# Attention of the second batch moved from the head into the first expert unit

## The chip, the cores and the metric

The kernel runs on one core of one Trainium2 chip. The metric is the device time of one execution in microseconds. Times before: 521.01 us median of three runs (519.59 to 523.30). The engines are called as the profile calls them: PE (TensorE; PEld is its weight load), DVE (VectorE), ACT (ScalarE), POOL (GpSimd), SP (SyncE, which issues most DMAs). Each engine works through its own instructions in order.

## The reference

Two blocks follow one another. The first is a cross attention between 512 tokens and 32 states for each of 8 batches and 8 heads of 64; it is computed both ways:

```python
scores  = scale * x @ state.T;   a  = softmax(scores);   xread = a  @ state    # tokens read states
scores2 = scale * state @ x.T;   a2 = softmax(scores2);  sread = a2 @ x        # states read tokens
out = concatenate([xread, sread], axis=2)          # 544 rows per batch and head
```

Its output, as 8 x 544 rows of 512, goes into a layer of 8 experts. A row takes the expert with its largest logit, or, where a local gate is open, the expert of the row before it in the batch; the first row of a batch always takes its own:

```python
e = fresh_e if s == 0 or local_gate[b, s] < 0.5 else prev_e
h = relu(x[b, s] @ w1[e]);   out[b, s] = softmax(logits[b, s])[e] * (h @ w2[e])
```

All is in fp32. One expert has 2 MB in `w1` (512 x 1024) and 2 MB in `w2`.

## The kernel before

**Units and tiles.** Each batch's 512 token rows are multiplied by the expert of that batch's first row: eight *units*. The 32 state rows of each batch go by their own experts: all 256 are sorted by expert into at most nine *tiles* of 32 rows (`Tile`, line 920), which need 2 MB + 2 MB of weights each. What fits neither is done at the end under a condition that does not come true with these data.

**A unit.** The two matrix products of a unit are done by a scheme of seven products of quarters instead of eight. It needs sums of the operands beforehand: four over the tokens (`column_sum`, line 842), four over the first weights (`first_sum`, line 831), four over the second (`second_sum`, line 847), all on DVE, line 829. A unit is two halves of the first multiplication (`first_half`, n = 0 and 1, products of line 1041) and two of the second (`second_half`, products of line 1088), each of seven products of eight matmuls: 28 products. The first product of a half needs no sums, the second needs the first sum of each kind. After each product `tick()` is called and whatever has been put at that number is issued: the order of the work beside the products is written out by hand in ticks. Unit u has ticks 28u + 1 to 28u + 28 (`PER = 28`). At the end of each half, places 4u to 4u + 3, `bound` may put in the first (`one`, line 950) or second multiplication (`two`, line 963) of a state tile.

**Attention.** A batch is a list of some 40 steps named by two letters: `sc` scores (PE, line 299), `tr` transposes to states and `mo` maxima over them, `sb`, `ex`, `zh`, `zs`, `zi`, `ml`, `tb` the softmax over states, `mx`, `nb`, `et`, `tu`, `ec`, `iv` that over tokens, `sr` state reads (PE, line 382, reads the rows `x_n`), `st`, `rt`, `ws`, `sl`, `sk` the state results, their rows to memory and their logits, `lg`, `lt` logits of tokens, `vv` token reads (PE, line 427), `xr`/`xd` their copies, `wr` their way to memory (`xts`), `fe` the first row's expert. `kp` are matmuls on zeros that keep PE going. `HEAD` gives the order for batches 0 and 1 ahead of the first unit; `FLOW` gives that of a batch b from 2 on, in ticks counted from `FIRST + PERIOD * (b - 2)`. Batch 0's token reads stay in SBUF as the first unit's tokens; for others `load_x` (line 822) reads them back from `xts`. A batch's tokens come in two layouts, `x_t` and `x_n`, 1 MB each, into one buffer each once the head is over.

**Routing.** `choose` (line 535) finds experts and probabilities for a group of batches in seven parts, put at seven ticks; its fourth part is a scan over 544 positions on DVE and its fifth takes the result to PE. `route` (line 607) sorts the states. Groups are batches 0 and 1, 2 to 4, 5 to 7.

**Queues.** SP issues in program order and waits in that order for what an issue needs. Writes to `out` go by indirect DMAs on POOL: for each half of the second multiplication two scatters of 128 rows (`scatter`, line 1023, data `y`), and one of line 972 for a tile (data `yt`, one buffer). Each waits for the one before it to land, except that the two scatters of the last half of all are declared independent of each other.

## Time and profile before

| | |
|---|---|
| median of three runs | 521.01 us (519.59 to 523.30) |
| profiled execution | 519.18 us |
| its span, first to last instruction | 516.9 us |
| granted PE clock, mean | 0.993 |
| busy: PE, DVE, ACT, POOL | 495.2, 278.1, 161.1, 109.3 us |
| moved by DMA | 115.67 MB, 224 GB/s over the span |
| first product of unit 0 | starts at 29.21 us |

A row of the order of time has the start in microseconds from the span's beginning, the duration, the engine, line and operation, what is written and read (names of tiles), shapes and count, and in brackets the idle time of the engine before it and what ended that. Rows in a row of the same kind are merged. A row of windows has the stretch, its length, busy time of PE, PEld, DVE, ACT and POOL with counts, the granted PE clock, the busy share of the DMA engines and GB/s. The chain of waits is the work that ended last, followed back from the end; its rows have start, length and what. The tile names that matter: `a` and `c` are a unit's first and second weights, `at` and `ct` a tile's; `xs` sums over tokens; `xr`, `x` token reads; `ps` and `sum` accumulators.

### The profile page before, as it was taken

Reading aid. Unit: us, or ns where it says so; the run is one execution under the profiler, and the core shown is the slowest. Engines: PE = TensorE matmul, PEld = TensorE weight load, DVE = VectorE, ACT = ScalarE, POOL = GpSimd, SP = SyncE. Lnnn points to the kernel's source line nnn. Section 1 sums busy time; section 2 is a strip of 40 time slices with the busy share of each in tenths; the row PEclk is TensorE's granted clock in tenths of the full one; section 3 lists DMA queues with packets and bytes.
Section 4 is the critical chain, followed back from the end, with each engine's and each line's share of the span. In section 5 each row is a group of like instructions: output and inputs, shape, how many; then the busy total and the mean of one; then the engine's idle time right before and its main releaser. Section 6 shows DMA issues by size and latency. Waiting matters only on the chain.

```text
span 516.9 us, 10104 instructions
## 1 busy us (share of the span) xinstructions
PE 495.2 (96%) x4008; PEld 392.3 (76%) x4008; DVE 278.1 (54%) x543; ACT 161.1 (31%) x334; POOL 109.3 (21%) x134
## 2 busy tenths in 40 slices
PE   8879999999999999999999999999999989989994
PEld 2438877787877778787888888888878878768884
DVE  4877967487655986436574944262513073403701
ACT  2623425244253442534222322332113221122220
POOL 4712123322133122320021002100212121011211
PEclk9989999999999999999999999999999999999998
DMA  8985282827739165451835774248999959997001
GB/s 311 346 283 215 84 331 92 306 98 234 281 114 316 64 234 182 121 191 41 285 121 163 286 255 167 83 169 309 414 355 377 364 227 406 368 368 295 8 20 67
DMA packets 38288, 115.67 MB, mean 224 GB/s; under 512 B 7748, under 2 KB 7880, under 8 KB 34008
## 3 DMA queue, kind: packets, MB, share of 16 engines
q1 hardware_dynamic: 34952, 105.37, 56.1%
q0 software_dynamic: 3136, 9.51, 4.9%
q8 instruction: 33, 0.54, 0.4%
q14 instruction: 23, 0.19, 0.1%
q10 hardware_dynamic: 144, 0.07, 0.1%
HBM read 97.10 MB, written 17.89 MB: 222 GB/s over the span
## 4 chain that ended last, share of the span: by engine, by line
PE 71%; DMA 17%; DVE 6%; issue 2%; ACT 1%; SPq 0%; POOLq 0%; POOL 0%; DVEq 0%
PE ps L1041 17%; PE ps L1088 17%; PE sum L1041 14%; PE sum L1088 12%; DMA out_dram<-y,tok 8%; DMA x<-xts 5%; DMA out_dram<-yt,row 3%; PE p L427 3%; PE s L299 2%; PE p L382 1%; PE p L369 1%; PE ps L963 1%; PE ps L950 1%; DMA x_t<-in_xt_dram 1%; DVE xs L829 1%
## 5 line engine op out<-in xcount | busy, mean ns | idle before, releaser
L1041 PE MATMUL ps<-x,a 128*128 128x256 f32 x384 | 92.3, 383 | 0.0
L1041 PE MATMUL sum<-xs,a 128*128 128x256 f32 x384 | 92.0, 382 | 0.0
L1025 POOL DMA_INDIRECT out_dram<-y,tok x32 | 36.6, 1144 | 230.6 <-DVE xs L829 59.1
L1041 PEld LDWEIGHTS sum<-xs,a 128*128 128x128 f32 x384 | 71.5, 190 | 16.5 <-ACT s L1070 4.1
L1041 PEld LDWEIGHTS ps<-x,a 128*128 128x128 f32 x384 | 71.7, 190 | 14.6 <-issue 5.2
L1088 PE MATMUL ps<-c,h 128*128 128x256 f32 x264 | 63.7, 384 | 0.0
L1088 PE MATMUL ps<-c,hs 128*128 128x256 f32 x256 | 60.8, 380 | 0.0
L1088 PE MATMUL sum<-c,h 128*128 128x256 f32 x248 | 58.6, 379 | 0.0
L1088 PEld LDWEIGHTS ps<-c,h 128*128 128x128 f32 x264 | 49.1, 190 | 8.9 <-issue 2.2
L1088 PEld LDWEIGHTS ps<-c,hs 128*128 128x128 f32 x256 | 48.4, 190 | 9.0 <-issue 2.5
L1088 PEld LDWEIGHTS sum<-c,h 128*128 128x128 f32 x248 | 46.7, 190 | 6.1
L829 DVE TENSOR_TENSOR a<-a,a 128x1024 f32<-128x1024 f32 x32 | 40.2, 1296 | 0.8 <-issue 0.6
L829 DVE TENSOR_TENSOR c<-c,c 128x1024 f32<-128x1024 f32 x32 | 38.4, 1241 | 0.3
L1041 PE MATMUL ps<-xs,a 128*128 128x256 f32 x128 | 31.2, 388 | 2.8 <-DVE a L829 2.8
L1070 ACT COPY s<-sum 128x512 f32<-128x512 f32 x32 | 18.8, 586 | 46.4 <-PE sum L1041 34.8
L1088 PE MATMUL sum<-c,hs 128*128 128x256 f32 x128 | 30.9, 384 | 0.0
L829 DVE TENSOR_TENSOR h<-s,s 128x512 f32<-128x512 f32 x16 | 11.0, 689 | 35.1 <-ACT s L1070 35.1
L1088 PEld LDWEIGHTS sum<-c,hs 128*128 128x128 f32 x128 | 23.8, 190 | 8.0 <-issue 2.5
L829 DVE TENSOR_TENSOR y<-s,s 128x256 f32<-128x256 f32 x16 | 6.8, 424 | 42.6 <-ACT s L1092 42.6
L1041 PEld LDWEIGHTS ps<-xs,a 128*128 128x128 f32 x128 | 24.7, 193 | 6.6 <-DVE a L829 3.2
L982 ACT COPY sum<-ps 128x512 f32<-128x512 f32 (+1 forms) x32 | 14.8, 464 | 47.3 <-PE ps L1041 23.8
L1092 ACT ACTIVATE s<-sum,prob 128x256 f32<-128x256 f32 x32 | 15.2, 474 | 45.4 <-PE sum L1088 44.2
(186 smaller groups left out, 561.5 us busy)
## 6 DMA issues: line engine op xcount, KB each, us to landing
at<-in_w_dram SPq DMA_DIRECT2D x18, 1024.0 KB
ct<-in_w_dram SPq DMA_DIRECT2D x18, 1024.0 KB
a<-in_w_dram SPq DMA_DIRECT2D x32, 512.0 KB
c<-in_w_dram SPq DMA_DIRECT2D x32, 512.0 KB
x_t<-in_xt_dram SPq DMA_DIRECT2D x16, 512.0 KB
x_n<-in_xn_dram SPq DMA_DIRECT2D x8, 1024.0 KB
xts<-xr SPq DMA_DIRECT2D x28, 256.0 KB
x<-xts SPq DMA_DIRECT2D x7, 1024.0 KB
```

What stands on the lines that cost most here:

```text
L299: self.nc.tensor.matmul(s[u][32 * k:32 * k + 32, :], lhsT=self.states(b)[r, k, :], rhs=self.get(f"x_t{k // 2}", b)[r, k % 2, :], start=Tru ...
L369: self.nc.tensor.transpose(t[:, q], self.get("e2", b, u)[:, q], self.route.ident)
L382: self.nc.tensor.matmul(r[32 * k:32 * k + 32, u, :], lhsT=e[:, c, u, 32 * k:32 * k + 32], rhs=x_n[:, c, u, k, :], start=(c == 0), stop=(c ...
L427: self.nc.tensor.matmul(v[k][SQ * j:SQ * j + SQ, :], lhsT=self.states_of[r, at:at + SQ], rhs=self.get("a", b, j // 2)[r, :], start=True, s ...
L829: self.nc.vector.tensor_tensor(out, a, b, op=op)
L950: nc.tensor.matmul(hps[SQ * g:SQ * g + SQ, :], lhsT=self.x_t[:, j, :], rhs=a[:, j, :, g], start=(j == 0), stop=(j == KT - 1))
L982: nc.scalar.copy(y, x)
L1025: put = nc.gpsimd.indirect_dma_start(out=out, out_offset=to, in_=y, in_offset=None, bounds_check=NT - 1, oob_is_err=False)
L1041: nc.tensor.matmul(to[:, m * width:m * width + width], lhsT=w[:, j, f:f + P], rhs=x[:, j, :], start=begin and m == 0 and j == 0, stop=(m = ...
L1070: return lambda t: nc.scalar.copy(to, t)
L1088: nc.tensor.matmul(to, lhsT=x[:, m, n * P:n * P + P], rhs=w[:, m, :], start=begin and m == 0, stop=(m == FK // 2 - 1), skip_group_check=True)
L1092: return lambda t: nc.scalar.activation(to, t, Act.Copy, scale=p)
```

## The change

- **Head.** `HEAD` now has batch 0 alone, up to its token reads. Of batch 1 only the scores and the transposes to states (`sc1`, `tr10`, `tr11`) are left. Batch 0's gates (`ga0`, `gk0`) and four `kp` matmuls come ahead of its scores, the other batches' gates behind them. All of `more_constants` (POOL and DVE), until now in tick 1, runs ahead of the scores. The gate weights come over ACT's queue, `x_n` of batch 1 is no longer loaded here.
- **Short chain.** For the first expert a chain of its own is built on the first 32 tokens' scores (`qa` to `qf`): transpose, maximum, exponential, shares, a product with the gates, a transpose, and the choice. At its end the first weights of unit 0 are loaded, and batch 2's `x_t` behind them.
- **Beside unit 0.** `BESIDE` puts the rest of batch 0 and batch 1 at ticks 1 to 21 of unit 0. Batch 1's reads go to memory in ticks 15 and 16, `load_x` and the first weights of unit 1 are issued in tick 17 (before: after the two first halves of unit 0, tick 14), batch 2's `x_n` in tick 18 (before: in the head). Token and weight sums of unit 1 lie in ticks 21 to 24 and 24 to 27 (before 18 and 22); the order of the sums ahead of unit 0 is changed.
- **Distance 12.** `FIRST, PERIOD` go from 2, 14 to 8, 12: batch 2's scores are in tick 8, its state reads in tick 23.
- **Groups.** Routing goes in four groups: batch 0; 1; 2 and 3; 4 to 7, with their ticks written out. The last ends in tick 107 (before 111), and `route` follows.
- **Tiles.** Their first multiplications are at places 17, 19, 20, 22, 23, 25, 26, 28, 29 (before 20 to 28), each second one place later, the last at 30. `at` has two buffers; a tile's first weights are loaded two tiles ahead, together with its rows, instead of one ahead.

```diff
 HEAD = """
-sc0 tr01 tr00 kp3 ga mo01 mo00 sb01 sc1 gl mx00 sb00 mx01 ex01 tr10 nb0 ex00 zh01 tr11 et00 zh00 zs01 mo10 et01 kp7
...
+ga0 kp4 gk0 sc0 tr00 tr01 ga1 kp4 mo01 mo00 gk1 sc1 sb01 qa mx01 sb00 qb ex01 qc zh01 ex00 mx00 kp6 qd zh00 zs01 zi01
+qe zs00 ml01 zi00 qf ml00 kp8 tb01 nb0 tb00 et00 tr10 vv00 et01 tr11 xr00 xd01 tu00 vv01 xr02 xd03 iv0 ec00
+"""
+
+BESIDE = """
+1 tu01 ec01 lg0 / 2 sr0 xn1 / 3 st0 lt0 mo11 sb11 / 4 rt0 sl0 mo10 sb10 mx10 / 5 sk0 mx11 nb1 ex11 / 6 zh11 ex10 et11 ws0 /
+7 zh10 et10 zs11 wr00 wr01 / 8 zi11 ml11 tu11 zs10 zi10 / 9 iv1 ec11 ml10 tu10 wr02 wr03 / 10 ec10 tb11 / 11 tb10 /
+12 lg1 / 13 lt1 vv10 / 14 xr10 xr11 fe1 / 15 vv11 wr10 wr11 / 16 xr12 xr13 sr1 wr12 wr13 / 18 st1 xn2 / 19 ws1 rt1 /
+20 sl1 / 21 sk1
 """
...
-FIRST, PERIOD = 2, 14
+FIRST, PERIOD = 8, 12
 PER = 28
-BEGIN = 20
+GROUPS = {(0, 1): (6, 7, 8, 9, 11, 12, 14), (1, 2): (22, 23, 24, 25, 26, 28, 30),
+          (2, 4): (49, 50, 51, 52, 61, 62, 64), (4, 8): (98, 99, 101, 102, 104, 105, 107)}
+ONES = 17, 19, 20, 22, 23, 25, 26, 28, 29
...
+    def quick_scores(self):
+        nc, q = self.nc, self.q[0]
+        for u in range(G):
+            nc.vector.transpose(q[:, u], self.get("s", 0, u)[:, :SQ])
+        nc.vector.tensor_reduce(self.qm, q, axis=AX, op=Alu.max)
+        nc.vector.tensor_tensor(q, q, self.quick(), op=Alu.subtract)
...
+    def quick_exponents(self):
+        self.nc.scalar.activation(self.q[0], self.q[0], Act.Exp, scale=SCALE)
+
+    def quick_shares(self):
+        nc, (q, t), z = self.nc, self.q, self.qm
+        nc.vector.tensor_reduce(z, q, axis=AX, op=Alu.add)
+        nc.vector.tensor_scalar(z, z, 1e-9, None, Alu.add)
+        nc.vector.reciprocal(z, z)
+        nc.vector.tensor_tensor(q, q, self.quick(), op=Alu.mult)
+        nc.vector.transpose(t.rearrange("p u n -> p (u n)"), q.rearrange("p u n -> p (u n)"))
+
+    def quick_logits(self):
+        self.of["q"] = self.bank(SQ, SQ)
+        for u in range(G):
+            self.nc.tensor.matmul(self.of["q"], lhsT=self.gl[:, 0, u, :], rhs=self.q[1][:, u], start=(u == 0),
+                                  stop=(u == G - 1))
+
+    def quick_turned(self):
+        self.nc.vector.transpose(self.ql, self.of["q"])
+
+    def quick_expert(self):
+        self.route.first_experts(0, 1, self.ql[0:1, :E].rearrange("o (b e) -> o b e", b=1))
+        self.work.load(0, 0)
+        for h in range(2):
+            self.load_t(2, h)
...
-        for i in range(4):
-            self.column_sum(i)
-        for i in range(4):
-            self.first_sum(i)
+        for do, i in ((self.column_sum, 0), (self.column_sum, 1), (self.column_sum, 2), (self.first_sum, 0),
+                      (self.first_sum, 1), (self.first_sum, 2), (self.column_sum, 3), (self.first_sum, 3)):
+            do(i)
...
-            tile_at["at"] = ft.tile([P, KT, F], F32, name="at")
+            tile_at["at"] = [ft.tile([P, KT, F], F32, name=f"at{i}") for i in range(2)]
...
             def begin(self):
+                self.x_t, self.x_g, self.at = [tile_at[n][self.i % 2] for n in ("xt", "xg", "at")]
+                self.ct = tile_at["ct"]
+                self.load(0)
                 quarter(self.x_g, slots.state[:, self.i:self.i + 1], rows)
...
         def bound(at, behind):
-            if at + 1 in ones:
-                ones[at + 1].turned()
             if at in twos:
                 behind.append(twos[at].two())
                 if twos[at].i + 1 < NTILE:
                     tiles[twos[at].i + 1].load(1)
             if at in ones:
                 ones[at].one()
-                i = ones[at].i
-                if i + 1 < NTILE:
-                    tiles[i + 1].load(0)
-                if i + 2 < NTILE:
-                    tiles[i + 2].begin()
+                if ones[at].i + 2 < NTILE:
+                    tiles[ones[at].i + 2].begin()
...
+        at(17, loads, 1)
+        for (b0, b1), ticks in GROUPS.items():
+            self.steps(route.choose(start.bank, b0, b1), *ticks)
+        tick = max(max(t) for t in GROUPS.values()) + 1
         at(tick, tiles_begin)
```

More of the change, by code (lines that the diff above doesn't have):

```diff
@@ L200, in __init__ @@
         self.parity = 0
+        self.q = [once.tile([P, G, SQ], F32, name=f"q{i}") for i in range(2)]
+        self.qm = once.tile([P, G], F32, name="qm")
+        self.ql = once.tile([SQ, SQ], F32, name="ql")
         self.zero = once.tile([P, 512], BF16, name="zero")
@@ L283, in gates @@
             r = slice(64 * u, 64 * u + 64)
-            for b in range(B):
+            for b in range(1, B) if i else range(1):
                 for k in range(KT):
@@ L873, in run @@
         places, load, index, add, xs = self.places, self.load, self.index, self.add, self.xs
-        for h in range(2):
-            start.load_t(2, h)
-        start.load_n(2)
-        load(0, 0)
         fc = ctx.enter_context(tc.tile_pool(name="fc", bufs=1))
@@ L1144, in unit @@
                 bound(U * u + n, waiting)
-            if ahead:
-                self.load_x(u + 1)
-                load(u + 1, 0)
+            if u and ahead:
+                loads(u + 1)
             behind = []
```

95 lines of the change are left out of this document (48 added, 47 removed).

## The prediction

> **What bounds the kernel now.** I read the page, then the order of time of the first 80 us, the chain of waits, the groups, and the order of time from 340 us on. The page gives the span:
>
> ```profile
> span 516.9 us, 10104 instructions
> ```
>
> The profiled execution took 519.18 us, so 2.3 us lie around the span; the median of the three runs, 521.01, is 1.8 above it. From the second product on, TensorE (PE) works nearly without a break. So the time is three things: how late the second product starts, how much TensorE work lies behind it, and the few places where TensorE waits. In the order of time of the head (start, duration, engine, line):
>
> ```profile
> 7.86 1.31 DVE L326 STREAM_TRANSPOSE e<-s 128x512 f32<-128x512 f32 x2 [6.61 <-PE s L299]
> ...
> 19.33 0.14 DVE L527 TENSOR_REDUCE first<-lt 1x1 f32<-1x8 f32 x1
> ...
> 20.91 1.94 SPq L819 DMA_DIRECT2D a<-in_w_dram  x4
> ...
> 30.21 0.67 DVE L829 TENSOR_TENSOR xs<-x 128x512 f32<-128x512 f32 x1
> ...
> 32.73 4.75 DVE L829 TENSOR_TENSOR a<-a,a 128x1024 f32<-128x1024 f32 x4
> ...
> 34.00 2.85 PE L1041 MATMUL ps<-xs,a 128*128 128x256 f32 x8 [2.79 <-DVE a L829]
> ```
>
> VectorE (DVE) begins with the scores at 7.86. The first expert is sought from 19.33 and its weights are asked for at 20.91, 1.58 us later. The sums over the tokens start at 30.21, when VectorE is through with batch 1; the first sum over weights starts at 32.73, and the second product, which needs it, at 34.00 after a wait of 2.79 us. That wait has a sequel, seen in a window of the clock and in the chain (start, length, what):
>
> ```profile
> 34.00:38.60 4.60, 4.60 (x25) 2.11 (x25) 4.53 (x12) 0.59 (x1) 0.00 (x0) 0.63 0.86 249
> ```
>
> ```profile
> 34.00 2.85 PE ps L1041 x8
> 36.85 1.78 PE s L299 x16
> 38.63 1.92 PE sum L1041 x8
> ...
> 42.28 1.73 PE sum L1041 x8
> ...
> 65.90 1.02 PE s L299 x16
> ...
> 93.19 3.65 PE ps L1041 x16
> ...
> 155.05 3.65 PE ps L1041 x16
> ```
>
> The granted clock was 0.63 in that stretch. The product took 2.85 us where one behind an insertion takes 1.92, the scores 1.78 where they take 1.02: 1.7 us lost. An undisturbed product is 1.73 us, so an insertion costs its own time and 0.2 on the next product. Unit 1 runs from 93.19 to 155.05, 61.86 us, with 28 products (48.44) and two batches of attention: 6.7 us of TensorE per batch.
>
> **The change part by part.** *The start.* Behind 7.86 the new head is one row of VectorE work; its prices are in the groups (form, count | busy, mean ns):
>
> ```profile
> L326 DVE STREAM_TRANSPOSE e<-s 128x512 f32<-128x512 f32 x16 | 11.0, 697 | 6.8 <-PE s L299 6.6
> L329 DVE TENSOR_REDUCE m<-e 128x16 f32<-128x512 f32 x16 | 10.7, 671 | 0.0
> L932 DVE STREAM_TRANSPOSE xtt<-xgt 128x128 f32<-128x128 f32 x9 | 2.7, 304 | 0.3 <-DMA xgt<-rows,state 0.3
> ```
>
> Up to the second product VectorE has, in the order of the new list: two transposes and two maxima over states (2.7), ten small steps of the short chain and its sums, each between 0.14 (the 1x8 row at 19.33) and 0.30 (a 128x128 transpose), 0.2 taken (2.0), two maxima over tokens (1.3), sums and inverses of the shares (1.3), the first expert (0.9 of the 1.58), four transposes (2.8), two copies of reads (1.3), the inverse (0.3), three token sums (2.0; four took 30.21 to 32.73) and one weight sum (1.2): 15.8 us. It begins 0.4 later than 7.86, because batch 0's gates and four idle matmuls now stand ahead of the scores, and it waits about 1.3 for the second half of the token reads, whose banks must first be copied out. The second product starts at 25.4 instead of 34.00: **-8.6**.
>
> The weights can hold it up. The expert is sought at about 15.8 and the load issued 1.58 later, at 17.4. How soon a load lands is bounded by this pair in unit 0, and its rate by a window:
>
> ```profile
> 60.31 0.33 SPq L822 DMA_DIRECT2D x<-xts  x1
> 65.53 1.35 DVE L829 TENSOR_TENSOR xs<-x 128x512 f32<-128x512 f32 x1 [0.39 <-DMA x<-xts]
> ```
>
> ```profile
> 70.00:72.00 2.00, 2.00 (x10) 1.77 (x10) 0.75 (x2) 0.16 (x1) 0.00 (x0) 1.00 1.02 404
> ```
>
> One MB issued at 60.31 ended a wait at 65.5: 5.2 us; 404 GB/s move in a full queue. The first sum needs three quarters of the weights, 1.5 MB: 5.2 + 1.2 = 6.4, so 23.8, a little before VectorE asks at 24.2. The queue is emptier than before, because batch 2's tokens now come behind the weights. The clock loss goes as well (**-1.7**): the gap before the second product shrinks to 1 or 2 us, since the first product, transposes and logits fill it. Bounds of the start: -9.5 to -5.
>
> *Work moved behind the second product.* Batch 1's attention but for its scores (6.7 - 1.2 = 5.5), and batch 0's state reads and state logits, about a quarter of a batch (1.7): **+7.2**. In the old head it ran in gaps of TensorE, here it is on the path; no cover exists. VectorE, ScalarE and GpSimd get the same work later. That token reads and scores of neighbouring batches fall on one tick at a distance of 12 saves some 0.5, and I leave 0.5 for waits on the denser VectorE; the two cancel.
>
> *Four routing groups for three.* The parts on TensorE are seen here, with transposes of attention as a price for below:
>
> ```profile
> 45.66 0.38 PE L566 MATMUL p<-identb,top 128*2 128x128 bf16 x4
> ...
> 46.08 1.99 PE L1041 MATMUL sum<-xs,a 128*128 128x256 f32 x8
> ...
> 52.08 0.25 PE L582 MATMUL p<-identb,ran 2*128 2x2 bf16 x4 [0.55 <-DVE ran L572]
> ...
> 52.67 1.99 PE L1041 MATMUL sum<-xs,a 128*128 128x256 f32 x8
> ...
> 56.23 0.60 PE L369 MATMUL p<-ident,e 128*128 128x128 f32 x4
> 56.66 1.89 PE L1041 MATMUL sum<-xs,a 128*128 128x256 f32 x8
> ```
>
> 0.42 + 0.59 and twice 0.2: **+1.4**. The wait of 0.55 on the scan may move, with batch 1's group one product behind its scan, but not by much.
>
> *State tiles.* TensorE's waits late in the trace:
>
> ```profile
> 383.52 1.93 PE L950 MATMUL ps<-at,xtt 128*32 128x256 f32 x32 [0.78 <-DMA at<-in_w_dram]
> ...
> 397.67 1.96 PE L963 MATMUL ps<-ct,htt 128*32 128x128 f32 x64
> 399.44 1.91 PE L950 MATMUL ps<-at,xtt 128*32 128x256 f32 x32
> ...
> 415.35 2.25 PE L963 MATMUL ps<-ct,htt 128*32 128x128 f32 x57 [1.71 <-issue]
> ...
> 418.16 1.93 PE L950 MATMUL ps<-at,xtt 128*32 128x256 f32 x31
> ...
> 451.31 1.93 PE L950 MATMUL ps<-at,xtt 128*32 128x256 f32 x32 [1.16 <-DMA at<-in_w_dram]
> ...
> 459.16 0.18 PE L709 MATMUL ps<-todo,ones 128*1 128x40 bf16 x1 [2.27 <-DVE todo L708]
> ```
>
> 0.78 and 1.16 on tile weights; 1.71, and 2.81 instead of 1.77 for the 64 matmuls behind it (2.75 together); 2.27 on VectorE: 7.0 us. Two of these hang on one chain:
>
> ```profile
> 354.44 12.65 DMA x<-xts
> ```
>
> ```profile
> 414.55 0.35 DVE L967 TENSOR_SCALAR yt<-ps,probq 128x128 f32<-128x128 f32 x1 [14.50 <-DMA out_dram<-yt,row]
> ```
>
> A unit's tokens landed 12.65 us after their issue, behind 4 MB of tile weights; VectorE, in order, stood at the token sums, the scatters were late, and VectorE then stood 14.50 us until the scatter of the previous tile had landed and its single buffer was free. Nine tiles over 13 places instead of 9, and a second weight buffer, put at most 2 MB before the tokens. I take back 6.0 of 7.0; two to seven is possible. Now only four places hold both halves of two tiles where eight did, which is four insertions more (+0.8): **-5.2**.
>
> *The tail.* The last tile's second half moves to the place before the last half of the last unit. Its scatter is then issued on GpSimd between the last two token scatters:
>
> ```profile
> 506.97 0.49 DVE L1100 SCALAR_TENSOR_TENSOR y<-ps,prob,s 128x256 f32<-128x256 f32 x1 [9.94 <-PE ps L1088]
> ...
> 508.24 0.98 POOL L1025 DMA_INDIRECT out_dram<-y,tok  x1 [3.70 <-DVE y L1100]
> ...
> 511.12 0.98 POOL L1025 DMA_INDIRECT out_dram<-y,tok  x1 [1.90 <-DVE y L1106]
> ```
>
> ```profile
> DMA to landing us min/median/max: 2.7/2.9/3.4
> ```
>
> The scatter at 508.24 was issued 0.78 after its data (506.97 + 0.49), behind the landing of the one before. Only the last two token scatters are declared independent, of each other; the tile's is not. So it waits for the one at 508.24 (2.9 to land, 0.78 to issue: 511.9), and the last one, queued behind it on GpSimd, waits for it in turn: 515.6 instead of 511.12, **+4.5** with nothing left to hide it. Were only the second of these two waits real, the last would follow one landing behind 509.2: +2; with none, 0.
>
> *Batch 2's rows.* They were loaded in the head. Now they are asked for in tick 18, behind batch 1's tokens and 2 MB of weights in tick 17, which wait for batch 1's reads to be written (tick 16), and state reads of batch 2 need them in tick 23. From tick 16 = t: copies and issue about one product (1.7), landing like a scatter's 2.9, the tokens 5.2, three MB more at 0.404 MB/us 7.4: t + 17.2. TensorE is there after seven products, state reads (1.2), two sets of transposes (0.43 each, 56.23 to 56.66) and logits (0.4): t + 14.6. A wait of 2.6 if the queue never runs empty, 5 if the write lands like a 1 MB load; I take **+3.5**. Everything behind it on TensorE waits too. After the 2.79 us wait of the head the clock fell, at 1.7 us; a wait of 3.5 should do the same, **+1.5**.
>
> On that the Trainium skill is harder to please: "TensorE: Matmul & The Clock Gate", Part 1, throttles after an idle window of about 3.4 us that runs freely, so that a gap of 3.5 need not fill one; by the page the 1.5 would mostly fall away, and the sum would be 1.1 instead of 2.6. The trace has a loss after 2.79 us, and I keep the row.
>
> **Sum:** -8.6 - 1.7 + 7.2 + 1.4 - 5.2 + 4.5 + 3.5 + 1.5 = +2.6. The profiled execution lies below all three runs, so I add it to the middle between it and the median, 520.1: **522.7 us**, no change that can be told (1% is 5.2 us, about what a measurement of this kernel can tell).
>
> **The rivals.** *Faster: the two new waits are not there.* The tile's scatter goes out at once, and batch 2's rows arrive in time because the loads of tick 17 start earlier. For it: the queue is lightly loaded at that point in the old unit 0. Against it: the old last scatters visibly wait for a landing, and loads land in the order of issue (the 12.65). 522.7 - 4.5 - 5.0 = 513.2. One of the two alone gives 518, no change.
>
> *Slower: the end of unit 0 hangs on batch 1's tokens.* They land at t + 9.8, and VectorE asks in tick 21, t + 11.1: 1.3 us in hand. If the write to memory takes 3 us more, token sums, weight sums and batch 2's shares, all in order on VectorE, are late by 2, the routing scan of tick 25 reaches TensorE late in tick 26, and the wait for batch 2's rows grows by the same 3: 3 + 2 = 5 more, 528. It decides from about 1.3 us of lateness on; against it, a scatter of the same size lands in 2.9.
>
> *No earlier start.* The short chain is itself VectorE work in the same queue. If the expert is known no earlier than before (issue 20.91), the third quarter lands at 27.3 and the second product starts at 28.6: 3.2 less gained, 525.9, at the edge of no change.
>
> **How the numbers follow.** Forecast, with one of its two waits missing included: 0.50. Both missing: 0.20. End of unit 0 slower: 0.22. No earlier start: 0.08, half of it beyond 1%. So faster by over 1% (below 515.8) 0.20, within 1% 0.54, slower (above 526.2) 0.26. The range for 8 in 10 goes from just under the fast rival to just over the slow one, 512 to 530; the forecast's own is 517 to 527.
>
> **What would show it.** Start: the second product near 25.4 and a clock near 1 behind it. Batch 2: the first state reads in tick 23 with a wait on rows of 2 to 5 us, and a dip of the clock. Tiles: no wait on tile weights, and TensorE's waits behind 320 us under 2 us. Tail: three scatters one after the other, each some 3.7 us behind the last, and 13 us from the scatter that stands at 508.24 to the end of the span instead of 8.7. The prediction is wrong if the second product starts after 28, if batch 2's state reads do not wait, or if the tail has its old length.

## The result, and the profile after

The changed kernel takes 538.96 us (median of four runs, 538.76 to 539.11) where the kernel before took 522.15 beside it: 1.0324 times as long, 95% interval 1.0274 to 1.0375. Forecast were 522.7 us, no change; the range ended at 530. The execution that was profiled took 539.11 us:

```profile
core 0: 537.3 us, clock 0.974
```

The span is 20.4 us longer (516.9 before) and the mean granted clock fell from 0.993 to 0.974. Spread evenly over the span, 0.7% of 516.9 (3.6 us) would be lost before and 2.6% of 537.3 (14.0 us) after, so that at most 10.4 of the 20.4 us are TensorE at half clock. Less of it was lost to work, because the mean counts the time in which TensorE stands still as well (0.52 between 530 and 537 us, without a matmul). Behind the second product the slow rows shown below are 6.5 us longer together than at full clock; in the kernel before it was 1.7.

Where the time went is read from the starts of the first product of each unit, in TensorE's order of time (line 1088 of the new kernel has the first half's products, 1135 the second's; a unit begins where 1088 follows 1135). All differences below are made from such starts:

| stretch | before | after | difference | predicted |
|---|---|---|---|---|
| to the second product | 34.0 | 29.2 | -4.8 | -8.6 |
| unit 0 from there | 59.1 | 70.3 | +11.2 | units 0 to 3: +11.9 |
| unit 1 | 61.9 | 72.7 | +10.8 | |
| units 2 and 3 | 118.5 | 117.3 | -1.2 | |
| units 4 to 7 | 236.8 | 237.5 | +0.7 | -5.2 |
| behind the last product | 6.6 | 10.2 | +3.6 | +4.5 |

Units 2 and 3 are as before, so the 22 us of units 0 and 1 are not attention that merely comes earlier; and the tiles gave nothing where 5.2 were expected. TensorE's waits in the new kernel (line, released by, total, times, longest):

```profile
PE ps L766 <- DVE todo L765: 4.4, 1, 4.4
PE p L439 <- DMA x_n<-in_xn_dram: 3.7, 1, 3.7
PE p L623 <- DVE top L614: 3.5, 1, 3.5
PE p L484 <- issue: 2.9, 1, 2.9
PE p L339 <- DVE q L334: 2.0, 1, 2.0
```

The last two stand in the head. Of the three behind it only the second was in the prediction. Each of these rows in its place, and a shorter wait in unit 0, with the product behind it (1.99 us where the clock is whole), in the order of time:

```profile
57.99 1.08 PE L484 MATMUL p<-a,states_of 32*32 32x512 f32 x14 [0.67 <-DVE undone L648]
59.01 3.55 PE L1088 MATMUL sum<-xs,a 128*128 128x256 f32 x8
...
86.86 2.01 PE L439 MATMUL p<-x_n,e 128*32 128x64 f32 x64 [3.75 <-DMA x_n<-in_xn_dram]
88.80 2.57 PE L1135 MATMUL sum<-c,hs 128*128 128x256 f32 x8
...
157.13 0.38 PE L623 MATMUL p<-identb,top 128*2 128x128 bf16 x4 [3.51 <-DVE top L614]
157.54 3.11 PE L1135 MATMUL sum<-c,hs 128*128 128x256 f32 x8
160.45 2.50 PE L1135 MATMUL ps<-c,h 128*128 128x256 f32 x8
...
472.18 0.18 PE L766 MATMUL ps<-todo,ones 128*1 128x40 bf16 x1 [4.44 <-DVE todo L765]
472.29 3.66 PE L1088 MATMUL sum<-xs,a 128*128 128x256 f32 x8
```

The head, in VectorE's and SP's order of time and TensorE's last rows:

```profile
8.91 1.31 DVE L383 STREAM_TRANSPOSE e<-s 128x512 f32<-128x512 f32 x2 [2.31 <-PE s L356]
...
17.59 0.97 DVE L586 SCALAR_TENSOR_TENSOR near<-near,iof 1x8 f32<-1x8 f32 x1
...
19.64 1.94 SPq L876 DMA_DIRECT2D a<-in_w_dram  x4
...
22.07 2.10 PE L484 MATMUL p<-a,states_of 32*32 32x512 f32 x16
24.11 3.78 PE L1088 MATMUL ps<-x,a 128*128 128x256 f32 x8
27.87 2.49 DVE L886 TENSOR_TENSOR a<-a,a 128x1024 f32<-128x1024 f32 x2 [0.64 <-DMA a<-in_w_dram]
29.22 1.99 PE L1088 MATMUL ps<-xs,a 128*128 128x256 f32 x8
```

The weights are asked for at 19.64, only 1.3 us earlier than before, and the first sum over them waits for them until 27.87. The token reads (2.10 for 16 matmuls that take 1.09) and the first product (3.78) run at half clock (granted 0.50 from 22 to 28 us); the second product is back at 1.99.

And the end, GpSimd's last scatters:

```profile
524.99 0.97 POOL L1072 DMA_INDIRECT out_dram<-y,tok  x1 [5.85 <-DVE y L1147]
528.29 0.97 POOL L1019 DMA_INDIRECT out_dram<-yt,row  x1 [2.34 <-DMA out_dram<-y,tok]
532.01 0.97 POOL L1072 DMA_INDIRECT out_dram<-y,tok  x1 [2.75 <-DMA out_dram<-yt,row]
```

Three scatters, each behind the landing of the one before, 12.3 us from the first of them to the end of the span.

### The profile page after: what moved, and what is told of

Its sections match the earlier page's. It is cut to its first block, busy times and chain, and to the rows that moved or that the text cites. A ratio compares the mean times of both kernels' runs of the same rounds, so it can differ in the third digit from the quotient of the medians.

```text
span 537.3 us, 10157 instructions
## 1 busy us (share of the span) xinstructions
PE 506.6 (94%) x4030; PEld 399.1 (74%) x4031; DVE 284.9 (53%) x574; ACT 160.8 (30%) x338; POOL 109.1 (20%) x134
## 4 chain that ended last, share of the span: by engine, by line
PE 82%; DMA 7%; DVE 6%; issue 2%; ACT 1%; POOL 0%; POOLq 0%; ACTq 0%; DVEq 0%
PE ps L1088 19%; PE ps L1135 19%; PE sum L1088 15%; PE sum L1135 14%; PE p L484 3%; PE ps L997 3%; DMA out_dram<-y,tok 3%; PE ps L1010 3%; DMA x_n<-in_xn_dram 2%; DMA out_dram<-yt,row 2%; PE p L439 2%; PE p L426 1%; DMA wgs<-in_wg_dram 1%; PE s L356 1%; DVE c L886 1%
## 5 line engine op out<-in xcount | busy, mean ns | idle before, releaser
L1088 PE MATMUL sum<-xs,a 128*128 128x256 f32 x384 | 95.1, 392 | 0.0
L1088 PE MATMUL ps<-x,a 128*128 128x256 f32 x384 | 94.1, 389 | 0.0
L1088 PEld LDWEIGHTS sum<-xs,a 128*128 128x128 f32 x384 | 73.9, 195 | 18.5 <-issue 7.5
L1088 PEld LDWEIGHTS ps<-x,a 128*128 128x128 f32 x384 | 72.9, 193 | 16.4 <-issue 5.0
L1072 POOL DMA_INDIRECT out_dram<-y,tok x32 | 35.4, 1107 | 232.7 <-DVE xs L886 42.0
L886 DVE TENSOR_TENSOR c<-c,c 128x1024 f32<-128x1024 f32 x32 | 40.0, 1279 | 2.6 <-DMA c<-in_w_dram 2.3
L886 DVE TENSOR_TENSOR a<-a,a 128x1024 f32<-128x1024 f32 x32 | 38.5, 1227 | 0.8 <-DMA a<-in_w_dram 0.6
L1135 PE MATMUL sum<-c,hs 128*128 128x256 f32 x128 | 32.4, 398 | 0.0
L886 DVE TENSOR_TENSOR xs<-x 128x512 f32<-128x512 f32 x16 | 10.9, 684 | 35.1 <-DMA x<-xts 35.1
L1135 PEld LDWEIGHTS sum<-c,hs 128*128 128x128 f32 x128 | 24.9, 198 | 4.5 <-issue 1.0
```

The lines of the kernel that those rows point to most:

```text
L886: self.nc.vector.tensor_tensor(out, a, b, op=op)
L1072: put = nc.gpsimd.indirect_dma_start(out=out, out_offset=to, in_=y, in_offset=None, bounds_check=NT - 1, oob_is_err=False)
L1088: nc.tensor.matmul(to[:, m * width:m * width + width], lhsT=w[:, j, f:f + P], rhs=x[:, j, :], start=begin and m == 0 and j == 0, stop=(m = ...
L1135: nc.tensor.matmul(to, lhsT=x[:, m, n * P:n * P + P], rhs=w[:, m, :], start=begin and m == 0, stop=(m == FK // 2 - 1), skip_group_check=True)
```

## The experiments

The theory after this comparison: each wait that the change adds to TensorE costs its own length and a stretch at half clock behind it, and each hangs on one chain that can be cut by itself. The rival: at a distance of twelve products VectorE has no time left, so that a wait taken away comes back at the next place. Line numbers in a run's rows are those of its own kernel, which an edit may have moved by a few lines. The start varies by almost 3 us between executions (second products from 28.5 to 31.2 in runs with the same head), so the verdicts below go by the stretch that the edit touches, beside the median.

**Batch 2's rows asked for first.**

```diff
-15 vv11 wr10 wr11 / 16 xr12 xr13 sr1 wr12 wr13 / 18 st1 xn2 /
+15 vv11 wr10 wr11 / 16 xr12 xr13 sr1 xn2 wr12 wr13 / 18 st1 /
```

> Batch 2's rows are asked for in tick 16, right behind batch 1's state reads, instead of tick 18 behind the tokens and weights of tick 17; nothing else changes. Theory (each new wait of TensorE costs its own length and a stretch at half clock): the wait of 3.75 us ahead of the state reads in tick 23 goes, and so do the 0.9 us that the reads and 0.7 us that the next product took too long: about -5.3 us against the changed kernel, 533.7. Rival (at twelve products' distance VectorE is what is late, and a wait that is removed comes back at the next place): under half of that is gained, 537 or more, with a new wait on VectorE within 15 us behind.

542.7 us, 1.0413 times the kernel before (1.034 to 1.0485): slower than the change itself. The wait on the rows is gone, and a longer one has come three products later (order of time, SP, VectorE, TensorE):

```profile
76.13 0.32 SPq L879 DMA_DIRECT2D x<-xts  x1
80.97 0.69 DVE L886 TENSOR_TENSOR xs<-x 128x512 f32<-128x512 f32 x1 [3.62 <-DMA x<-xts]
95.72 0.26 PE L639 MATMUL p<-identb,ran 1*128 1x1 bf16 x4 [5.19 <-DVE ran L629]
```

SP waits for the state reads before it can ask for the rows, the reads of batch 1 behind that go to memory later, `load_x` is issued at 76.13 instead of 72.25, VectorE waits 3.62 us for the tokens, and the routing scan, which stands behind in VectorE's order, holds TensorE for 5.19. So this one load cannot be moved ahead in SP's order: VectorE has no slack for batch 1's tokens. That was the prediction's slower rival, with 1.3 us in hand. In hand there was nothing: the tokens landed 4.84 us after their issue here, which in the change would be 77.09, and there VectorE takes them up at 77.16.

**The state reads later instead.**

```diff
+                    late = 3 if b == 2 and name in ("sr", "st", "ws", "rt") else 0
-                    at(FIRST + PERIOD * (b - 2) + int(tick), self.named, name, b)
+                    at(FIRST + PERIOD * (b - 2) + int(tick) + late, self.named, name, b)
...
-            at(FIRST + PERIOD * (b - 3) + 16, self.load_n, b)
+            at(FIRST + PERIOD * (b - 3) + (19 if b == 3 else 16), self.load_n, b)
```

> Batch 2's state reads, and the copies and transposes that follow from them, stand three products later (tick 26 instead of 23); batch 3's rows are asked for three later as well. Loads stay where they are, so the tokens of batch 1 are as early as in the changed kernel. Theory (a wait costs its length and a stretch at half clock, and the run with the rows asked for first lost because it made the tokens 3.9 us late for VectorE, which has no slack in unit 0): the wait of 3.75 us and the slow stretch of 1.6 us go, and at most 1.5 us come back as a wait on the routing scan in tick 26: -4 us against the changed kernel, 535. Rival (VectorE is what bounds unit 0 whatever the rows do): the scan's wait grows to 4 us or more, unit 0 keeps its 70.3 us, 538 or more.

534.2 us, 1.0266 (1.0236 to 1.0296). Unit 0 takes 64.6 us. Two other runs of this head kept the full clock behind the wait of 0.67 us, as this one did, and there unit 0 takes 68.2 (e6_last_tile_apart) and 68.5 us (e4_two_yt). The reads have no idle time in front of them (87.01, 1.10 us), and the scan's wait is as forecast:

```profile
89.57 0.25 PE L640 MATMUL p<-identb,ran 1*128 1x1 bf16 x4 [1.46 <-DVE ran L630]
```

The wait on the rows cost what it seemed to cost; here the theory holds, and in the run before it was the order of SP's issues that spoilt it.

**Unit 2's token sums later.**

```diff
-                    at(PER * u + 18 + i if u else 21 + i, self.column_sum, i)
+                    at(PER * u + (20 if u == 1 else 18) + i if u else 21 + i, self.column_sum, i)
```

> The four token sums for unit 2 stand two products later (ticks 48 to 51 instead of 46 to 49); the routing group stays. If the 3.51 us that TensorE waits for the routing of batches 2 and 3 come from VectorE's own wait of 4.71 us on unit 2's tokens, that wait shrinks to 1 us or none, the routing is ready in time, and the wait on TensorE goes with its slow stretch (1.2 and 0.6 us on two products): -5.3 us, 533.7. If VectorE is simply short of time in unit 1, its work comes later still and the wait on TensorE stays above 2.5 us: 538 or more.

540.49 us, 1.0361 (1.0276 to 1.0446), no gain. In the changed kernel VectorE had waited for the tokens; here it waits at the next instruction that needs another engine, and is at the same place at the same time (order of time, VectorE of the changed kernel, then of this run, then TensorE of this run):

```profile
141.45 0.69 DVE L886 TENSOR_TENSOR xs<-x 128x512 f32<-128x512 f32 x1 [4.71 <-DMA x<-xts]
```

```profile
145.90 0.42 DVE L886 TENSOR_TENSOR y<-s,s 128x256 f32<-128x256 f32 x1 [4.65 <-ACT s L1139]
...
148.35 0.48 DVE L1147 SCALAR_TENSOR_TENSOR y<-ps,prob,s 128x256 f32<-128x256 f32 x1 [2.02 <-PE ps L1135]
...
150.25 3.23 DVE L886 TENSOR_TENSOR xs<-x,xs 128x512 f32<-128x512 f32 x1
...
156.78 0.17 DVE L614 SCALAR_TENSOR_TENSOR top<-lt,own 128x10 bf16<-128x10 f32 x1
...
157.01 0.38 PE L623 MATMUL p<-identb,top 128*2 128x128 bf16 x4 [3.51 <-DVE top L614]
```

So the 4.71 us of waiting on tokens were not the cause. What is: between 148.35 and 156.95 VectorE works without a break, 8.6 us, and the routing's first part, put at tick 49, is the last of it; TensorE wants its result in tick 51, two products later. The wait is a lead of two products against a queue of 8.6 us. Of these, 2.6 us are one token sum, which takes 3.23 us beside GpSimd (row at 150.25) and 0.63 to 0.69 otherwise; the change has the same row at 150.37. No run took this stretch alone away, so how much of the wait hangs on it stays open.

**The routing group later.**

```diff
-          (2, 4): (49, 50, 51, 52, 61, 62, 64),
+          (2, 4): (49, 50, 54, 55, 61, 62, 64),
```

> The routing of batches 2 and 3 keeps its first two parts (ticks 49, 50); its transposes on TensorE and the scan behind them stand three products later (ticks 54, 55 instead of 51, 52). Theory: TensorE no longer waits there, VectorE keeps its wait of 4.71 us on the tokens, which is hidden: -5.3 us, 533.7, the same as with the sums moved. Rival (VectorE short of time): the next thing that TensorE needs from VectorE in unit 1 or early in unit 2, the shares' transposes or the weight sums, shows a new wait of over 2 us, and less than half is gained.

539.9 us, 1.0354 (1.0259 to 1.0448). The wait of 3.51 is gone; 0.55 and 1.56 have come, the second ended by ScalarE's copy out of the accumulators. Unit 1 takes 70.6 us (72.7 in the change, 73.7 in most runs): 2 to 3 us gained where the theory had 5.3 and the rival less than half; the new wait of over 2 us that the rival named did not come either. The second product came 2 us later in this execution, which hides it in the total.

**Two buffers for a tile's result.**

```diff
-                y = tile_at["hp"].tile([P, P], F32, name="yt")
+                y = tile_at["hp"].tile([P, P], F32, name="yt", bufs=2)
```

> A second buffer for a state tile's result on its way to memory; nothing else changes. Theory (the chain of scatters): VectorE stands 10.7 us at the tile's scaling in unit 7 because the one buffer is held until the scatter of the tile before has landed, three scatters after one another at over 6 us each; with two buffers that wait goes, the cast of the undone list is in time, and TensorE's wait of 4.44 us and the 1.8 us of the slow product behind it go: -6 us, 533. Rival (the tokens' late landing is the cause: VectorE waits 11.1 us on unit 7's tokens just before): the wait on the undone list stays above 2 us.

534.26 us, 1.0259 (1.0186 to 1.0332). Unit 7 takes 56.9 us instead of 63.0: -6.1, as the theory said, and the list of waits has no row on the undone list any more. VectorE's row of the tile's scaling, in the change and in this run:

```profile
471.69 0.35 DVE L1014 TENSOR_SCALAR yt<-ps,probq 128x128 f32<-128x128 f32 x1 [10.69 <-DMA out_dram<-yt,row]
```

```profile
463.45 0.35 DVE L1014 TENSOR_SCALAR yt<-ps,probq 128x128 f32<-128x128 f32 x1 [3.16 <-PE ps L1010]
```

The second buffer takes away a wait for the landing of the previous tile's scatter, which had itself waited 6.16 us for a token scatter to land (the last row of this document).

**The last tile's scatter independent.**

```diff
+                if self.i == NTILE - 1:
+                    tc.declare_no_dep(put.ins, group="scatters", reason="a state has one slot, so scatters write other rows")
+                    tc.add_to_no_dep_group("scatters", put.ins)
```

> The last state tile's scatter is declared independent of the two last token scatters, as those two are of each other; all instructions and their order stay. Theory (three scatters wait for one another's landing): the wait of 2.34 us of the tile's scatter and of 2.75 us of the last one go, and the end comes 9 us instead of 12.3 us behind the issue of the scatter before: -3.4 us, 535.5. Rival (the last stretch is set by the last product and the writing of its result): no difference, 539.

535.28 us, 1.0305 (1.0256 to 1.0353). From the last product to the end of the span it is 6.5 us, as in the kernel before, instead of 10.2:

```profile
522.59 0.97 POOL L1075 DMA_INDIRECT out_dram<-y,tok  x1 [5.85 <-DVE y L1150]
523.87 0.97 POOL L1019 DMA_INDIRECT out_dram<-yt,row  x1 [0.30 <-issue]
525.48 0.97 POOL L1075 DMA_INDIRECT out_dram<-y,tok  x1 [0.64 <-DVE y L1156]
```

No wait on a landing is left between them. -3.7 us in that stretch: the prediction's term of the end is right in kind, and 0.8 too large.

**The short chain first in the head.**

```diff
-ga0 kp4 gk0 sc0 tr00 tr01 ga1 kp4 mo01 mo00 gk1 sc1 sb01 qa mx01 sb00 qb ex01 qc zh01 ex00 mx00 kp6 qd zh00 zs01 zi01
-qe zs00 ml01 zi00 qf ml00 kp8 tb01 nb0 tb00 et00
+ga0 kp4 gk0 sc0 qa tr00 qb tr01 ga1 kp4 qc mx01 gk1 sc1 qd kp6 qe qf mo01 mo00 sb01 sb00 ex01 zh01 ex00 mx00 zh00 zs01 zi01
+zs00 ml01 zi00 ml00 kp8 tb01 nb0 tb00 et00
```

> Only the order of the head changes: the short chain to the first expert stands on VectorE ahead of the transposes' maxima and of every GpSimd operation of batch 0, so that none of its steps runs beside one. The amount of work is the same. Theory: the steps that took 0.50 to 1.12 us instead of 0.15 to 0.2 were stretched by GpSimd running beside them; alone they are short, the expert is known near 13 and the weights are asked for near 14 instead of 19.6. VectorE's work up to the weight sums then bounds the second product, at 26.5 to 27.5 instead of 29.2: -2 us in all, 537. Rival A (the weights' landing alone set the second product): 24 to 25, -4 us or more. Rival B (no stretch by GpSimd): the steps stay as long, the weights are asked for at 16 or later.

539.09 us, 1.033 (1.0283 to 1.0376): no gain. The steps of the chain are short now, and the weights are asked for at 15.99:

```profile
10.58 0.31 DVE L318 STREAM_TRANSPOSE q<-s 128x32 f32<-128x32 f32 x2 [3.93 <-PE s L356]
11.18 0.22 DVE L320 TENSOR_TENSOR q<-q,qm 128x64 f32<-128x64 f32 x1
...
15.99 1.94 SPq L876 DMA_DIRECT2D a<-in_w_dram  x4
22.45 1.96 PE L484 MATMUL p<-a,states_of 32*32 32x512 f32 x16 [5.22 <-DVE a L420]
...
30.33 2.48 DVE L886 TENSOR_TENSOR a<-a,a 128x1024 f32<-128x1024 f32 x2
31.97 1.99 PE L1088 MATMUL ps<-xs,a 128*128 128x256 f32 x8
```

The subtraction of 0.22 us took 1.12 in the change (12.04 us into the span), and a 1x8 step of 0.15 (14.76) took 0.97 (17.59), while GpSimd had a subtraction and a multiplication of 128x512 under way. So the stretch is real, 2.4 us over four steps. But 5.4 us from VectorE's first row to the request of the weights, where it was 10.7, did not bring the second product nearer: it comes 21.4 us behind VectorE's first row, 20.3 in the change. The weights are waited for no more; now batch 0's own chain through VectorE, GpSimd, ScalarE and TensorE is last, with 5.22 us of TensorE's idling in it. Both rivals fall, and so does the theory's size.

**The clock kept in the head.**

```diff
-ex00 mx00 kp6 qd     ...  ml00 kp8 tb01
+ex00 mx00 kp14 qd    ...  ml00 kp20 tb01
```

> More idle products on TensorE in the head, 14 instead of 6 ahead of the short chain's logits and 20 instead of 8 ahead of the token reads; nothing else. Theory: TensorE's gaps of 2.0 and 2.9 us close, the granted clock stays near 1 through the first products, the second pair of token reads takes 1.1 us instead of 2.1 and the first product 1.9 instead of 3.8; the copies behind the reads come 1 us earlier, and the weights' landing then holds VectorE: second product at 28.5 to 29, and what is behind it another 1 us earlier: -1.5 us, 537.5. Rival (the gaps do not cost): the first product still takes over 3 us, no difference.

539.42 us, 1.033 (1.0284 to 1.0375): no gain. The first product takes 1.99 us and the token reads 1.24, as forecast; then the weights are late for VectorE, and the gap and the slow product are only moved behind them (TensorE and VectorE in order of time):

```profile
25.49 1.99 PE L1088 MATMUL ps<-x,a 128*128 128x256 f32 x8 [0.48 <-DMA a<-in_w_dram]
29.54 3.62 DVE L886 TENSOR_TENSOR a<-a,a 128x1024 f32<-128x1024 f32 x3 [1.48 <-DMA a<-in_w_dram]
30.82 3.38 PE L1088 MATMUL ps<-xs,a 128*128 128x256 f32 x8 [2.33 <-DVE a L886]
```

From VectorE's first row (10.44) to the second product it is 20.4 us, as in the change. With e7 this says that the start hangs on two chains that end close together, in the change within 0.64 us, the wait at 27.87: the weights, and batch 0's attention. Cutting one shows the other. No run cut both, so what the start would then be is not shown.

**The tiles alone.** The kernel before, with the change's tiles only:

```diff
-BEGIN = 20
+ONES = 18, 19, 20, 22, 23, 25, 26, 28, 29
...
-            tile_at["at"] = ft.tile([P, KT, F], F32, name="at")
+            tile_at["at"] = [ft.tile([P, KT, F], F32, name=f"at{i}") for i in range(2)]
...
+                self.load(0)
```

> The kernel before with only the change's part on state tiles: two buffers for a tile's first weights, loaded when the tile begins, nine tiles over places 18, 19, 20, 22, 23, 25, 26, 28, 29 instead of 20 to 28 (the first stands one later than in the change, since the tiles' list is ready later here). My prediction's steps: -5.2 on the tiles and +4.5 at the end, -0.7. Theory after the first comparison: waits on tile weights and the 2.75 us at 415 go (-4.7), the wait on the undone list grows from 2.3 to 4.4 with a slow product behind it (+3.9), four more insertions (+0.8), the end +3.6: +3.6 us against the kernel before, about 525.5. Rival (the tiles' part is neutral, and the changed kernel's late loss comes from the denser attention): 522, with the end as long as before.

522.34 us, 1.0038 (1.0015 to 1.0062): 2 us slower. Units 4 to 7 take 236.2 us where the kernel before takes 236.8; the stretch behind the last product 10.3 where it takes 6.6. The stall in unit 7 is there without the denser attention (VectorE, then TensorE), and the last two scatters wait 2.33 and 2.71 us for landings, as in the change:

```profile
454.18 0.35 DVE L968 TENSOR_SCALAR yt<-ps,probq 128x128 f32<-128x128 f32 x1 [10.32 <-DMA out_dram<-yt,row]
454.67 0.18 PE L709 MATMUL ps<-todo,ones 128*1 128x40 bf16 x1 [4.08 <-DVE todo L708]
```

**The kernel before with mended tiles.** The tiles of the run above, with the second buffer of e4_two_yt and the independent scatter of e6_last_tile_apart.

> The kernel before (its head, 14 products for each batch's attention, three routing groups) with the change's tiles as in the run of the tiles alone, a second buffer for a tile's result, and the last tile's scatter declared independent of the last two. Theory (the tiles' part is good but for the chain of scatters): unit 7 loses the wait of 4.1 us and the slow product (-6 against the tiles alone), the end is 6.5 us behind the last product (-3.7): 522.3 - 9.7 = 512.6, 1.5% faster than the kernel before. Rival (the waits move into units 5 or 6, where the tokens land as late as before): 516 or more.

514.76 us, 0.9881 times the kernel before (0.9837 to 0.9925): faster than both. Unit 7 takes 56.9 us and the end 6.5, as expected; the span is 512.7, and 2 us lie around it. The granted clock is 0.993.

**The change with all of it mended.** The edits of e5_reads_later, e4_two_yt, e6_last_tile_apart and e12_clock_kept, and unit 2's sums in another way:

```diff
-                    at(PER * u + 18 + i if u else 21 + i, self.column_sum, i)
-                    at(PER * u + 22 + i if u else 24 + i, self.first_sum, i)
+                    at((21 + i, (46, 47, 51, 52)[i], PER * u + 18 + i)[min(u, 2)], self.column_sum, i)
+                    at((24 + i, 52 + i, PER * u + 22 + i)[min(u, 2)], self.first_sum, i)
```

> The changed kernel with batch 2's state reads three products later, unit 2's last two token sums behind the routing group's first part and its weight sums two products later, two buffers for a tile's result, the last tile's scatter independent, and more idle products in the head (14 and 20 instead of 6 and 8). Every wait of TensorE behind the head that the changed kernel added is then taken away. Theory: 64.6 us for unit 0, 68.4 for unit 1, 57 for unit 7, 6.5 at the end, the head 1 us shorter: 537.3 - 5.7 - 4.5 - 6.1 - 3.7 - 1 = a span of 516, about 518, the same as the kernel before, since 8.6 us of TensorE's work were moved behind the second product for 5 us of an earlier start. Rival (VectorE is short of time at twelve products): new waits in units 0 to 2, unit 1 at 71 or more, 523 or more.

524.94 us, 1.0061 (1.0027 to 1.0095): what the rival said (523 or more), and slower than the kernel before. Its profiled execution took 530.42 us, 5.5 more than the median, so its waits say where TensorE stood rather than what it usually costs:

```profile
PE p L640 <- DVE ran L630: 3.4, 1, 3.4
PE ps L1092 <- DVE a L887: 2.4, 1, 2.4
PE p L624 <- DVE top L615: 2.3, 1, 2.3
```

The scan in unit 0 and the routing's first part in unit 1 still come late from VectorE, and the second product waits for its weight sum. Ahead of the scan and ahead of the routing's part stands a step stretched beside GpSimd: a weight sum of 3.83 us at 87.96 where others take 1.2, and a 1x8 step of 2.98 us at 153.47 where it takes 0.15. In unit 1 the token sum was out of the way, the stretch fell on another step, and a wait stayed. The theory of chains that can be cut singly holds for the tiles, the end and the rows, and not for units 0 and 1 as a whole.

**Fourteen products again.**

```diff
-FIRST, PERIOD = 8, 12
+FIRST, PERIOD = 8, 14
...
-          (2, 4): (49, 50, 51, 52, 61, 62, 64), (4, 8): (98, 99, 101, 102, 104, 105, 107)}
-ONES = 17, 19, 20, 22, 23, 25, 26, 28, 29
+          (2, 4): (51, 52, 53, 54, 63, 64, 66), (4, 8): (108, 109, 111, 112, 114, 115, 117)}
+ONES = 20, 21, 22, 23, 24, 25, 26, 28, 29
```

> The changed kernel with each batch's attention again 14 products behind the one before instead of 12; the routing of batches 2 and 3 keeps its lead of two products (now ticks 51 to 54), that of the last four comes ten later, and the tiles start at place 20 instead of 17. Theory (the wait on the routing comes of its short lead, not of the density): TensorE still waits 2 to 4 us on the routing in tick 53, and of unit 1 only the third batch's part (5 us) moves to the units behind: the sum over units 1 to 3 falls by under 3 us. Rival (density): that wait is under 1 us, and units 1 to 3 together are 6 us shorter or more.

538.03 us, 1.0316 (1.0266 to 1.0367). The theory falls here: with the same lead of two products the wait on the routing is gone (TensorE, no idle time in front of it),

```profile
158.75 0.38 PE L623 MATMUL p<-identb,top 128*2 128x128 bf16 x4
```

and units 1 to 3 take 184.5 us instead of 190.0, a little under the rival's 6. Three steps of VectorE in front of the routing were stretched here too, by 2.7 us together, so the stretch alone does not make the wait. The kernel is hardly shorter all the same: units 4 to 7 take 241.2 us instead of 237.5, with waits of 2.63 and 1.30 us ahead of first multiplications of tiles, which start three places later, and unit 0 took 1.7 more.

**The head alone, and the density alone**, each beside the mended tiles. The first is the changed kernel with `FIRST, PERIOD = 8, 14`, the ticks of the run above, tiles from place 19, and the edits of e5, e4 and e6; the second is e9 with one line:

```diff
-FIRST, PERIOD = 2, 14
+FIRST, PERIOD = 2, 12
```

> The kernel before with mended tiles, and of the change's other parts the head alone (short chain, batch 1 beside the first unit, four routing groups, with batch 2's state reads three products later): each batch's attention is 14 products behind the one before, as in the kernel before. Theory (the head itself loses, waits or not): second product 29.2 instead of 34.3 (-5.1), unit 0 at 64.6 instead of 59.1 (+5.5), units 1 to 3 together 184.5 instead of 180.4 (+4.1, the work that starts six products later), then as in the kernel before with mended tiles: 512.7 + 4.5 = a span of 517, about 519. Rival (the head is worth its 5 us once the density is undone): 512 or less.

> The kernel before with mended tiles, and of the change's other parts the distance of 12 products alone (old head, attention from product 2 on, three routing groups with their old leads). Theory (density costs through VectorE where a routing group falls into it): TensorE's work is the same, only earlier; a wait of 2 to 4 us with a slow stretch behind it comes at the routing of batches 2 to 4 in unit 1 or 2, and units 0 to 3 take 239.5 + 4: 519. Rival (density as such is free, and the changed kernel's loss in unit 1 hangs on the short lead of its routing alone): units 0 to 3 take 239.5 within 1.5 us, 514 to 516.

The head alone: 523.26 us, 1.0026 (0.9994 to 1.0059), against 0.9881 without it, so it costs 1.45% or 7.6 us. By stretches: start -4.9, unit 0 +7.2, units 1 to 3 +6.3 (186.7 against 180.4). That is 4 us more than the theory had, and 3.1 of them are two products at half clock (3.39 and 3.65 us) behind waits of 0.67 and 0.84 us. The density alone: 515.92 us, 0.9875 (0.9823 to 0.9928), against 0.9881: nothing in all, as the rival said. By stretches it is more than that: units 0 to 3 take 242.3 us, 2.8 more than without it, which is nearer to the theory's 243.5 than to the rival's 239.5 within 1.5, and units 4 to 7 take 3.0 less. A wait on the routing comes there too. It is short, but the product behind it takes 3.50 us:

```profile
162.56 0.39 PE L566 MATMUL p<-identb,top 128*3 128x128 bf16 x4 [1.24 <-DVE top L557]
```

So the head is what loses, and the density costs nothing in all beside the old head. Under the new head it brought the wait of 3.51 us, which the run with fourteen products does not have; which part of VectorE's load makes that difference was not separated.

## Why the prediction was wrong

The sum gave +2.6 us and the span became 20.4 longer. Of the 17.8 us between, 3.8 are the start, 8.9 units 0 to 3 and 5.9 the tiles; the end gives 0.9 back.

**The start (-8.6).** Came as -4.8. Two steps failed. VectorE's chain was added up with each step at its price from before, 14.6 us of work and 1.3 of waiting up to the last token sum that is needed first. From 8.91 to that sum's end (27.2) it was 18.3, of which 2.4 are the four steps stretched beside GpSimd and 2.1 the wait for token reads at half clock. And the weights, to be asked for at 17.4 and there in 6.4 us, were asked for at 19.64 and took 8.2. The 6.4 was worked out from one MB's landing in unit 0 and a full queue's rate there, and neither row is from the head. That both chains ended close together is what the runs of the head showed.

**The clock at the start (-1.7).** Half right. Behind the second product the loss is gone: it takes 1.99 us where it took 2.85. But the gap was not closed, it became two, 2.0 and 2.9 us, ahead of the second product, and a loss stands there instead (2.10 and 3.78 us), inside the -4.8.

**Work moved behind the second product (+7.2).** Right. Summed over units 0 to 3, TensorE's time on the attention's steps (from start to next start, waits taken out) is 43.1 us in the run of the head alone and 35.3 in the kernel before: 7.8. **The fourth group (+1.4):** 1.0 by the same sums of the routing's steps in the change.

**Batch 2's rows (+3.5 and +1.5).** Right: a wait of 3.75, reads 0.9 and the next product 0.6 too slow. The Trainium skill ("TensorE: Matmul & The Clock Gate", Part 1) has the clock throttled after an idle window of about 3.4 us that runs freely, which a gap of 3.5 us need not fill. Here the gap cost the clock each time, in the change and in the seven other runs that kept this wait (3.22 to 3.95 us). The measurement decides.

**What was missing.** I let half a microsecond for a denser VectorE cancel against merged steps. This term failed. In its place stand the wait on the routing of batches 2 and 3, 3.51 us with 1.7 on the two products behind it, and a wait of 0.67 in unit 0 with 1.6 behind it. With these 7.5 the 11.9 of units 0 to 3 become 19.4; measured 20.8. The 1.4 that is left is spread over the attention's steps and the products behind them. The routing's ticks are in the diff, so VectorE's queue at that point could have been added up. Its stretched step could have been looked for as well: in the kernel before, a token sum took 2.23 us at 77.51, beside a GpSimd subtraction.

**The tiles (-5.2).** Wrong: +0.7, and -0.6 where the tiles were changed alone. I had booked 6.0 of 7.0 us of waits as gone, 2.27 of them on VectorE's undone list. The waits on weights did go: the rows of 0.78, 1.16 and 1.71 have no answer above 0.3. But the chain that I quoted for it, a tile's single result buffer behind scatters behind late tokens, was untouched by the change; its delay moved to the place where TensorE hangs on VectorE, 4.44 us and 1.7 of clock. The second buffer, which the change doesn't have, brings the 6.1.

**The end (+4.5).** Right in its mechanism, 3.6 measured, and taken away when one scatter was declared independent. From the scatter that corresponds to 508.24 to the end I expected 13 us; it is 12.3, since the landings were waited for 2.34 and 2.75 us instead of 2.9.

The rivals: the faster one had both new waits absent, and both were there. The slower one named the tokens of batch 1 as the point without slack; it did not act in the change itself, but the run that delayed them by 3.9 us showed that it would have. "No earlier start" is half true: the weights were asked for 1.3 us earlier, not 3.5.

## What to carry to other kernels

Moving work from a stretch with gaps to one without costs its whole length; it pays only by what the start of that stretch gains, and a start that hangs on several chains comes no sooner than the last of them: add up each to its end before counting on one. In an order written by hand, the lead of a step is to be measured in the work queued in front of it on its engine (8.6 us of VectorE here, 2.6 of them one step stretched beside GpSimd), not in products. A wait of 3.1 us or more on TensorE cost about 1.5 to 3 us more than it shows every time here, and a shorter one did so in some executions. When a wait vanishes, look which single buffer or which dependence stood behind it; here two such edits of a few lines took the tiles' part from 522.3 to 514.8 us, more than the change's own gain at the start.

## What was not expected of the hardware

**The same wait cost the clock in some runs only.** Twelve of the profiled kernels with the new head have the same wait of 0.67 us on the routing in unit 0, in the middle of 16 small matmuls. Windows of the clock behind it, in the change and in e4_two_yt (the third number from the end is the granted clock):

```profile
60.00:62.00 2.00, 2.00 (x6) 1.55 (x6) 1.97 (x5) 0.00 (x0) 0.00 (x0) 0.50 0.00 0
```

```profile
60.00:62.00 2.00, 2.00 (x11) 1.77 (x10) 2.00 (x5) 1.06 (x3) 0.00 (x0) 1.00 0.00 0
```

In seven of them (the change, e1, e2, e3, e10, e11, e13) the product behind took 3.1 to 3.7 us, in five (e4, e5, e6, e7, e12) 1.99. That is a large part of the 2 us by which unit 0 differs between runs with the same edits there. Of the 28 waits of 3.1 us or more that the profiles show behind 25 us, each was followed by a slow product (2.5 to 3.8 us). In between both occur: the wait of 2.79 us ahead of the second product had a slow one behind it in the kernel before and in two runs with its head, and one of 1.99 us in the run of the density alone. The Trainium skill, on the page cited above ("TensorE: Matmul & The Clock Gate", Part 1), says that the window runs freely and does not start with the kernel. That the same wait went either way agrees with it. That an idle window of about 3.4 us is needed does not agree: in the rows around the 0.67 us at most 1.7 us are idle.

**VectorE's steps with two inputs stretch beside GpSimd.** The short chain's subtraction took 1.12 us beside GpSimd's and 0.22 without; a token sum, otherwise 0.63 to 0.69, took 3.23 at 150.37 while GpSimd had a multiplication and a subtraction of 128x512 (150.98 to 153.05) under way. Transposes and reductions beside GpSimd kept their length. The Trainium skill says in "GPSIMD Engine Reference", 1. Specifications, that the SBUF interfaces are shared with VectorE, with contention for VectorE instructions with two SBUF inputs. The trace agrees. These two rows are five times as long; a 1x8 step, above, took 2.98 us instead of 0.15.

**A scatter landed later while weights were loading.** GpSimd waited 6.16 us at 465.09 for a scatter of 128 rows to land, issued 7 us before; from 458 to 465 us the DMA engines moved 272 GB/s at a busy share of 0.77. At the end it waited 2.34 and 2.75 us, with a busy share of 0.18 from 524 to 530 and 0.11 from 530 to 537. That the load is the cause was not tested by itself.

```profile
465.09 0.98 POOL L1019 DMA_INDIRECT out_dram<-yt,row  x1 [6.16 <-DMA out_dram<-y,tok]
```
